# Behind the last FFN tile: 836 further float32r matmuls of four widths, at changing byte offsets between their weights and their moving rows

## The chip, the cores and the metric

The kernel runs on one core of one Trainium2 chip. The metric is the device time of one execution in microseconds. Times of the kernel before: a median of 1186.85 us over 2 runs (1186.52 to 1187.18). One further execution was taken with the hardware profiler; all rows of the profile come from it.

## The reference

The kernel computes one transformer block on 2048 tokens of width 576, with attention and FFN in parallel. Cut to what matters:

```python
x = A_x                                    # (1, 2048, 576) float32
xn = layernorm(x)                          # over the 576 columns, eps 1e-5
qkv = xn @ wqkv                            # 32 heads of 18
o = attention over 8 keys at distances 0, 2, .. 14 behind each token
h = relu(xn @ w1 + b1) ** 2                # 576 -> 4608
out = x + o @ wo + h @ w2 + b2             # 4608 -> 576
```

## The kernel before

**Precision.** A float32 operand is split into a high part in float32r and a float32r rest (`split`, line 96), and a product is made of three matmuls: high by high, high by rest, rest by high. So nearly all work of TensorE is float32r matmuls, each of which appears in the profile as one weight load (engine PEld) and one matmul (engine PE). The first operand of `nc.tensor.matmul` after the destination is the stationary one (128 columns of weights), the second is the moving one, whose number of columns is called the width here.

**Tiling.** The tokens are worked in 4 blocks (`NB`) of 512 (`TB`), and the 4608 hidden columns in 36 tiles of 128 (`NF`). A step n from 0 to 144 (`NT` is 144) does one FFN tile of one block: `step` (line 496) loads the weights of tile n + 2, splits those of n + 1, does `ffn1(n)` and, two steps late (`LAG`), `ffn2(n - 2)`. In steps of its own, listed in `pre` and `mid`, stand the projections to q, k and v (`qkv`, line 243, by `three`, line 235) and the output projection (`o_chunk` and `o_acc`).

**The four widths.** `ffn1` (line 342) has 14 matmuls of width 512 for a tile; `three` (line 241) has 14 of width 432 (`3 * CG`) for 128 tokens; `accumulate` (line 367) has pairs of width 320 (`YA`) and 256 (`YB`), because the 576 output columns are cut into two PSUM segments. In the last step `ffn2_tail` (line 396) does the last two tiles segment by segment, so that there 320 follows 320 and 256 follows 256: for each of six segments it runs all matmuls, then a VectorE addition (`drain`, line 387) and an output DMA.

**Buffers that the change uses.** `raw1` holds the unsplit w1 tile (128 x 640 float32, three buffers, loaded in line 312). `xt` is a single buffer of 10,240 bytes a partition; the normalisation of a block uses it, the last time some steps ahead of the fourth block. `wk` is a pair of PSUM banks, taken in turn by `ffn1`, `three`, and `o_chunk`.

**What sets the order.** A scheduler orders the instructions of each engine from the program's text and its own estimates of time; each engine then runs its list in order, and semaphores hold it where data are missing. Loads and stores are issued by SyncE's queue (SPq in the profile). At the end of the program all engines meet in a barrier, once the last stores have landed.

Of the kernel before, what the change touches and what calls it, by code (L numbers as in the profile page):

```python
# [8 lines left out]
F32 = mybir.dt.float32  # L9
F32R = mybir.dt.float32r  # L10
BF16 = mybir.dt.bfloat16
AF = mybir.ActivationFunctionType
# [4 lines left out]
P = 128  # L17
S, D, F = 2048, 576, 4608
H, DH, W, DIL = 32, 18, 8, 2
TB = 512  # L20
NB = S // TB
NJ = TB // P
NC = 5
# [3 lines left out]
CG = HG * DH  # L27
# [4 lines left out]
YA, YB = 320, 256  # L32
# [8 lines left out]
def block_kernel(ctx: ExitStack, tc: tile.TileContext, x, xt, wqkv, wo, w1, b1, w2, b2, out):  # L41
# [454 lines left out]
    def step(n):  # L496
        if 2 < n + 2 < NT:
            load_w(n + 2)
        if n + 1 < NT:
            split_w1(n + 1)  # L500
        for f, a in pre.get(n, []):
            f(*a)
        if n < NT:
            ffn1(n)
            split_w2(n)
        busy = n >= NF and n % NF in (LAG - 1, LAG - 2)
        for f, a in mid.get(n, []):
            f(*a)
        if not busy:
            piece()  # L510
            piece()
        if n == NT:
            ffn2_tail([NT - 2, NT - 1])
        elif n >= LAG:
            ffn2(n - LAG)
        if not busy:
            piece()

    for n in range(NT + 1):
        with opening() if n < 3 else ExitStack():  # L520
            step(n)


_OUTS = [((1, S, D), 'float32')]

# [33 lines left out]
```

## Time and profile before

| | |
|---|---|
| median of 2 runs | 1186.85 us |
| the profiled execution's own time | 1186.68 us |
| its span, first to last instruction | 1184.6 us |
| PE busy | 1174.9 us, 99% of the span, 6930 matmuls |
| PEld busy | 1080.3 us, 91% |
| VectorE, ScalarE busy | 867.9 us (73%), 596.6 us (50%) |
| mean granted TensorE clock | 0.999 |

A row of the timeline has the start in us, the time it took, engine, line, operation, what is written and read, the shape and how many such instructions were merged into the row. Matmuls are pipelined: the record of one matmul is longer than the distance to the next one's start. What a matmul costs in a stream is therefore read as the distance between starts, or from the chain of waits, where a row gives start, length and number of a piece of work that follows without a gap. The mean ns in the list of groups is the length of the record.

### The profile page before, as it was taken

What the parts mean: (1) busy time and instruction counts of PE and PEld (TensorE: products, weight loads), DVE (VectorE), ACT (ScalarE), POOL (GpSimd) and SP (SyncE); (2) the same over time, 40 slices, a digit from 0 to 9 for tenths busy, and PEclk for the clock granted to TensorE, in tenths of its full rate; (3) what the DMA queues carried; (4) which work ended last, traced back from release to release, by engine and by line L of the source; (5) the groups of instructions that cost most, each with busy time, mean ns of one, the idle gap of its engine ahead of it and who ended that gap; (6) DMA issues with size and microseconds to landing.
All of it is one profiled execution on the core that took longest, in us unless ns stands there. A gap on an engine that the chain in (4) does not pass through costs nothing.

```text
span 1184.6 us, 17735 instructions
## 1 busy us (share of the span) xinstructions
PE 1174.9 (99%) x6930; PEld 1080.3 (91%) x6930; DVE 867.9 (73%) x1051; ACT 596.6 (50%) x1079; POOL 40.3 (3%) x47
## 2 busy tenths in 40 slices
PE   8999999999999999999999999999999999999998
PEld 5999999989999999999989999999999999999998
DVE  7399899882689795994288979598428895958432
ACT  6545445553536454555364545455535454445542
POOL 4003000000000200000000020000000000000000
PEclk9999999999999999999999999999999999999999
DMA  7556345332536554423264654533326434343311
GB/s 239 188 177 220 119 166 201 96 100 78 197 123 212 211 174 144 141 86 116 72 232 133 226 206 125 185 97 106 100 89 227 171 120 172 98 155 96 109 58 50
DMA packets 70164, 172.22 MB, mean 145 GB/s; under 512 B 8384, under 2 KB 20288, under 8 KB 69312
## 3 DMA queue, kind: packets, MB, share of 16 engines
q1 hardware_dynamic: 70080, 171.09, 43.5%
q8 instruction: 54, 0.88, 0.3%
q14 instruction: 30, 0.25, 0.1%
HBM read 156.81 MB, written 14.24 MB: 144 GB/s over the span
## 4 chain that ended last, share of the span: by engine, by line
PE 97%; DVE 2%; issue 0%; ACT 0%; DMA 0%; SPq 0%; POOL 0%; DVEq 0%
PE y L367 43%; PE wk L342 38%; PE wk L241 15%; DVE xt L185 1%; PE wk L202 1%; DVE wql L100 0%; DMA xb<-in_x 0%; SPq L89 0%; PE y L202 0%; DVE w2l L100 0%; DVE hl L349 0%; ACT r L344 0%; ACT hh L347 0%; DVE st L111 0%; DVE w1l L100 0%
## 5 line engine op out<-in xcount | busy, mean ns | idle before, releaser
L367 PE MATMUL y<-w2l,hh 128*128 128x256 f32 (+1 forms) x1152 | 253.1, 296 | 0.0
L367 PE MATMUL y<-w2h,hh 128*128 128x256 f32 (+1 forms) x1152 | 252.8, 297 | 0.0
L367 PE MATMUL y<-w2h,hl 128*128 128x256 f32 (+1 forms) x1152 | 251.8, 296 | 0.0
L342 PE MATMUL wk<-xh,w1h 128*128 128x512 f32 x720 | 213.9, 394 | 0.8 <-DVE kv L207 0.8
L367 PEld LDWEIGHTS y<-w2h,hh 128*128 128x128 f32 x1152 | 186.4, 189 | 7.6
L342 PE MATMUL wk<-xh,w1l 128*128 128x512 f32 x720 | 187.2, 390 | 2.0 <-DVE w1l L100 2.0
L367 PEld LDWEIGHTS y<-w2l,hh 128*128 128x128 f32 x1152 | 180.4, 189 | 1.9
L367 PEld LDWEIGHTS y<-w2h,hl 128*128 128x128 f32 x1152 | 179.8, 190 | 0.5
L98 ACT ACTIVATE w1h<-raw 128x640 fp32r<-128x640 f32 x144 | 106.1, 737 | 120.6 <-PE wk L342 114.6
L98 ACT ACTIVATE w2h<-raw 128x576 fp32r<-128x576 f32 x144 | 98.1, 682 | 134.7 <-PE y L367 134.7
L342 PEld LDWEIGHTS wk<-xh,w1l 128*128 128x128 f32 x720 | 135.1, 188 | 30.3 <-DVE w1l L100 2.3
L342 PE MATMUL wk<-xl,w1h 128*128 128x512 f32 x576 | 155.1, 390 | 0.0
L100 DVE TENSOR_TENSOR w1l<-raw,w1h 128x640 fp32r<-128x640 f32 x143 | 118.9, 832 | 47.7 <-PE wk L342 34.0
L100 DVE TENSOR_TENSOR w2l<-raw,w2h 128x576 fp32r<-128x576 f32 x144 | 110.8, 771 | 55.9 <-ACT w2h L98 55.8
L342 PEld LDWEIGHTS wk<-xh,w1h 128*128 128x128 f32 x720 | 126.2, 189 | 20.5 <-DVE kv L207 1.0
L303 DVE TENSOR_REDUCE qo<-pr 128x144 f32<-128x1152 f32 x64 | 138.8, 2169 | 0.6
L342 PEld LDWEIGHTS wk<-xl,w1h 128*128 128x128 f32 x576 | 108.0, 188 | 23.9
L349 DVE TENSOR_TENSOR hl<-r,hh 128x512 fp32r<-128x512 f32 x144 | 99.5, 691 | 34.1 <-ACT r L348 34.1
L344 ACT ACTIVATE r<-wk,b1t 128x512 f32<-128x512 f32 x144 | 98.5, 684 | 44.5 <-PE wk L342 44.1
L100 DVE TENSOR_TENSOR wql<-wqr,wqh 128x432 fp32r<-128x432 f32 x80 | 50.0, 642 | 95.5 <-ACT wqh L98 95.5
L241 PE MATMUL wk<-wql,xh 128*128 128x432 f32 x320 | 114.8, 359 | 0.0
L241 PE MATMUL wk<-wqh,xh 128*128 128x432 f32 x320 | 114.7, 359 | 0.0
(77 smaller groups left out, 1228.1 us busy)
## 6 DMA issues: line engine op xcount, KB each, us to landing
raw<-in_w SPq DMA_DIRECT2D x144, 320.0 KB, 2.9
raw<-in_w SPq DMA_DIRECT2D x144, 288.0 KB, 2.8
wqr<-in_wqkv SPq DMA_DIRECT2D x80, 216.0 KB, 4.5
kv<-kscr SPq DMA_DIRECT2D x16, 1008.0 KB, 5.3
kv<-vscr SPq DMA_DIRECT2D x16, 1008.0 KB, 7.5
raw<-in_wo SPq DMA_DIRECT2D x20, 288.0 KB, 2.7
kscr<-kv SPq DMA_DIRECT2D x16, 288.0 KB, 3.0
vscr<-kv SPq DMA_DIRECT2D x16, 288.0 KB, 3.4
```

The costliest lines, as they stand in the source:

```text
L98: nc.scalar.activation(hi, raw, AF.Copy)
L100: (only or nc.vector).tensor_tensor(out=lo, in0=raw, in1=hi.bitcast(F32), op=ALU.subtract)
L185: nc.vector.tensor_tensor(out=v, in0=v, in1=mb[b][:, :, k].rearrange("c p j -> c j p"), op=op)
L202: nc.tensor.transpose(p[:, j * P:(j + 1) * P], src[:, j, c * P:(c + 1) * P], ident)
L241: nc.tensor.matmul(ps, l, r, start=i == 0, stop=i == len(mm) - 1)
L303: nc.vector.tensor_reduce(out=q[:, j], in_=pr.rearrange("p w c -> p c w"), axis=AX.X, op=ALU.add)
L342: nc.tensor.matmul(p, l, r, start=i == 0, stop=i == len(mm) - 1)
L344: nc.scalar.activation(r, p, AF.Relu, bias=b1t[:, f:f + 1])
L349: last_hl[0] = nc.vector.tensor_tensor(out=hl, in0=r, in1=hh.bitcast(F32), op=ALU.subtract)
L367: nc.tensor.matmul(y, a[:, t * P:(t + 1) * P], w[:, c0:c1], start=first and i == 0 and opens, stop=last and i == len(pairs) - 1, skip_grou ...
```

## The change

Behind the last step the program gets a new function, called once. It copies the last w1 tile four times into one float32r buffer `t` of 2560 columns, on ScalarE, and then runs matmuls whose weights and moving rows both come from `t`. All write the same PSUM tile `a`, each with start and stop set, and nothing reads `a`. The tokens' output is not touched.

```diff
+    def offset_map():
+        t = sb.tile([P, NC * TB], F32R, name="xt", bufs=1)
+        for i in range(4):
+            nc.scalar.activation(t[:, i * 640:(i + 1) * 640], raw1[NT - 1], AF.Copy)
+        a = pw.tile([P, TB], F32, name="wk")
+
+        def row(w, m, n):
+            nc.tensor.matmul(a[:, :n], t[:, w // 4:w // 4 + P], t[:, m // 4:m // 4 + n],
+                             start=True, stop=True, skip_group_check=True)
+
+        for i in range(4):
+            row(2048, 0, TB)
+        for k in range(32):
+            w = 2048 + 64 * k
+            for n in (TB, 3 * CG, YA, YB):
+                for i in range(4):
+                    row(w, 0, n)
+            for i in range(3):
+                row(w, 0, YA)
+                row(w, 4 * YA, YB)
+        for k in range(8):
+            w = 2560 + 256 * k
+            for n in (TB, 3 * CG, YA, YB):
+                for i in range(4):
+                    row(w, 256, n)
+
+    offset_map()
```

`w` and `m` are byte offsets in a partition's row of `t`. In the first loop `w` takes 32 values, 64 bytes apart, and the moving rows start at 0 (or at 1280, for the second of a pair). In the second loop the moving rows start at 256 and `w` takes 8 values, 256 bytes apart.

In the instruction lists of the changed program, against those of the program before, the 836 matmuls (line 530) stand together at the end of TensorE's list, behind the last matmul of line 367. The four ScalarE copies (line 526) stand earlier: behind the activation of line 348 whose row begins at 1124.60 us in the profile before, ahead of the `w2h` split that begins at 1126.50 us. VectorE, GpSimd and SyncE have the same lists as before.

## The prediction

> **What bounds the kernel now.** First the head of the profile's page, its busy times, the clock, and the shares of the chain of waits; then the chain in order of time, where it shows which rows follow each other without a gap.
>
> ```profile
> span 1184.6 us, 17735 instructions
> PE 1174.9 (99%) x6930; PEld 1080.3 (91%) x6930; DVE 867.9 (73%) x1051; ACT 596.6 (50%) x1079; POOL 40.3 (3%) x47
> PEclk9999999999999999999999999999999999999999
> PE 97%; DVE 2%; issue 0%; ACT 0%; DMA 0%; SPq 0%; POOL 0%; DVEq 0%
> ```
>
> TensorE is busy for 99% of the span and is 97% of the chain, at full granted clock to the end. So a matmul that is put behind the last one isn't absorbed by a gap: it moves the end by its distance to the next start. The chain in order of time, around the steps that matter here and at the end:
>
> ```profile
> 740.46 5.47 PE wk L241 x28
> ```
>
> ```profile
> 1126.47 3.20 PE wk L342 x14
> 1129.67 3.20 PE y L367 x24
> 1132.86 0.44 PE wk L202 x4
> 1133.30 3.20 PE y L367 x24
> 1136.50 3.20 PE wk L342 x14
> 1139.70 3.19 PE y L367 x24
> ...
> 1169.35 11.74 PE y L367 x88
> 1181.10 0.02 issue
> 1181.12 0.49 DVE xb L387
> ```
>
> These rows already price three of the new kinds: width 432 costs 5.47 / 28 = 0.1954 us, width 512 costs 3.20 / 14 = 0.2286 us, and a pair of 320 and 256 costs 3.20 / 12 = 0.2667 us. For 320 behind 320 and 256 behind 256 I read the tail, in the timeline of PE:
>
> ```profile
> 1175.40 0.40 PE L367 MATMUL y<-w2h,hh 128*128 128x256 f32 x2
> ...
> 1176.84 0.31 PE L367 MATMUL y<-w2h,hh 128*128 128x320 f32 x1
> ...
> 1178.60 0.40 PE L367 MATMUL y<-w2h,hh 128*128 128x256 f32 x2
> ...
> 1180.77 0.31 PE L367 MATMUL y<-w2h,hl 128*128 128x320 f32 x1
> ```
>
> By the loops of `ffn2_tail`, 12 matmuls of 256 stand between the first two rows, 12 of 320 between the second and the third: 1.44 / 12 = 0.120 us and 1.76 / 12 = 0.1467 us. The last row is the last matmul of the kernel before; the next could start at 1180.77 + 0.147 = 1180.92.
>
> **A fixed part in every matmul.** From 256 to 320 columns the price grows by 26.7 ns, 0.417 ns a column. With that, 256 columns stream in 106.7 ns and the row of 0.120 us has 13.3 ns over; 320 has 13.3, 512 has 15.3 and 432 has 15.4. Within a group of width 512 it isn't constant:
>
> ```profile
> 1126.30 1.09 PE L342 MATMUL wk<-xh,w1h 128*128 128x512 f32 x4
> 1127.23 1.07 PE L342 MATMUL wk<-xl,w1h 128*128 128x512 f32 x4
> 1128.14 0.39 PE L342 MATMUL wk<-xh,w1h 128*128 128x512 f32 x1
> ```
>
> The first four take 0.93 / 4 = 232.5 ns each (19.2 over), the next four 0.91 / 4 = 227.5 ns (14.2 over). So the part over the stream is 13 to 19 ns and depends on how a load falls against the running matmul. By the built program's addresses the distance from moving rows to weights is a multiple of 256 bytes in all 6816 float32r matmuls of before, and in 308 of the 836 new ones (every fourth k of the first loop, the second loop, the first four). The other 528 (24 x 22) lie at 64, 128 or 192 bytes off that grid, which no row of before shows.
>
> **The 836 matmuls.** 4 + 32 x 22 + 8 x 16. Width 512: 4 + 128 + 32 = 164 x 0.2286 = 37.5 us. Width 432: 160 x 0.1954 = 31.3. Width 320 in fours: 160 x 0.1467 = 23.5. Width 256 in fours: 160 x 0.120 = 19.2. Pairs: 96 x 0.2667 = 25.6. Sum 137.0 us.
>
> For the 528 off the grid the bounds are: below, the whole fixed part of 13.3 ns goes (-7.0 us); above, it is paid twice (+7.0 us), a guess wider than any row. Nearest rows: width 432, whose stream ends off the grid, has 2.1 ns more than 256 and 320; the first four of a 512 group, not yet in step, 5.9 ns more. I take 4 ns, between those two: 528 x 4 = 2.1 us.
>
> **Weights that repeat.** Most new rows have their predecessor's weights. The list of groups shows that this saves no load: in `accumulate` a pair shares its weights, and yet has one load a matmul, 1152 loads for 576 + 576 matmuls.
>
> ```profile
> L367 PEld LDWEIGHTS y<-w2h,hh 128*128 128x128 f32 x1152 | 186.4, 189 | 7.6
> ```
>
> ```profile
> L367 PE MATMUL y<-w2h,hh 128*128 128x320 f32 x576 | 180.3, 313 | 0.0
> ...
> L367 PE MATMUL y<-w2h,hh 128*128 128x256 f32 x576 | 161.0, 281 | 0.0
> ```
>
> **A page on the fixed part.** The Trainium skill, TensorE: Matmul & The Clock Gate, says under "Step-by-step: what each phase is for" that TensorE has two independent SBUF read ports, so that loading the next weights doesn't take read bandwidth from the running matmul, and under "Back-to-back issue gap" gives 2.5 ns over the stream. By it the offset would be nothing, and the sum, an estimate, 125.2 (300,544 columns at 0.417 ns) + 836 x 0.0025 = 127.3 us. The rows above have 13 to 19 ns there, so the trace does not agree on the size; no row of before can show whether the offset is nothing, which is rival A below.
>
> **The four copies on ScalarE.** They wait for the last w1 load, and stand ahead of a `w2h` split:
>
> ```profile
> 1123.78 0.33 SPq L312 DMA_DIRECT2D raw<-in_w  x1
> ```
>
> ```profile
> raw<-in_w SPq DMA_DIRECT2D x144, 320.0 KB, 2.9
> ```
>
> ```profile
> 1124.60 0.63 ACT L348 ACTIVATE r<-r 128x512 f32<-128x512 f32 x1
> 1126.50 0.69 ACT L98 ACTIVATE w2h<-raw 128x576 fp32r<-128x576 f32 x1 [1.28 <-PE y L367]
> 1128.57 0.74 ACT L98 ACTIVATE w1h<-raw 128x640 fp32r<-128x640 f32 x1 [1.38 <-PE wk L342]
> 1129.70 0.69 ACT L344 ACTIVATE r<-wk,b1t 128x512 f32<-128x512 f32 x1 [0.39 <-PE wk L342]
> ```
>
> The load lands at about 1123.78 + 2.9 = 1126.7, the copies run to 1126.7 + 4 x 0.74 = 1129.7. Queued behind them: `w2h` (3.2 us late), `w1h` to 1131.1, r to 1131.8; then VectorE's `w1l`, by about 1132. First to need these is TensorE's next group of line 342 at 1136.50 (row above), for `w1h`, `w1l` and the bank of `wk` that r frees. Cover is 4 us or more, so the copies cost nothing; without it they would cost up to 3.2 us once. SyncE's, GpSimd's and VectorE's lists are not changed, and the new matmuls find `t` ready 50 us ahead.
>
> **The end.** Before, the last store sets it: issued at 1181.64, landing 2.1 us later, 0.9 us ahead of the span's end of 1184.6.
>
> ```profile
> 1181.64 0.34 SPq L410 DMA_DIRECT2D out<-xb  x1
> ```
>
> ```profile
> out<-xb SPq DMA_DIRECT2D x2, 160.0 KB, 2.1
> ```
>
> The last additions and stores now run beside the new matmuls, so 3.7 us behind 1180.92 stop counting. After: 1180.92 + 137.0 + 2.1 (off grid) + 0.16 (the last record is 281 ns long, its distance counted at 120) + 0.9 = 1321.1 us of span. The profiled execution took 1186.68 us, 2.1 more than its span: 1323.2. It stands 0.2 under the median of the runs shown: **1323.4 us**.
>
> **The rivals.**
> - *A, the offset does nothing*: off-grid rows cost what the others do, 1323.4 - 2.1 = 1321.3 us. For it: settled 512 rows have 14 ns wherever on the grid they lie. Against it: no row lies off the grid.
> - *B, off-grid rows are cheaper*: loads and stream stop meeting and up to 13.3 ns fall away in 528 rows, down to 1314.3 us. Against it: in the rows the part over the stream is never under 13.
> - *C, off-grid rows pay the fixed part twice or more*: 1328.3 us and above. For it: the parts of 13 to 19 ns already vary with how a load falls.
> - *D, repeated weights are not loaded again*: the fixed part is gone nearly everywhere, 1321.3 - 836 x 0.0133 = 1310.2 us. The pairs above speak against it.
> - *E, not slower*: `a` is read by nobody; if the matmuls were dropped on the way to the chip, the copies alone would be left and the time stays at 1186.9 us. It decides at the count of PE: 6930 or 7766. The built list has all 836. To hide instead, they would have to fit in the 3.7 us under the last stores, 4.4 ns each, where the cheapest row has 120.
> - *F, the clock halves* in the new stretch: 137 us more, about 1460 us. The clock's row has full speed throughout, and nothing separates the new matmuls from the old.
>
> **How the numbers follow.** Forecast (off-grid rows 2 to 6 ns dearer, 1322.4 to 1324.6): 0.40. A: 0.26. B: 0.14. C: 0.15. D: 0.02. E: 0.01. F: 0.02. The range is 1315 to 1330 us: it takes in the forecast, A, nearly all of B, whose bottom needs every meeting to vanish, and the part of C up to 1.25 times the bound of +7.0 us. Left out are D, E, F, and what of B and C lies beyond: about 0.15. Faster by over 2%: no case, put at 0.00. Within 2% (under 1210.6 us): E, 0.01. Slower by over 2%, which is about what a measurement of this kernel can tell from no change: 0.99.
>
> **What would show it.** Right: PE x7766 and PEld x7766; line 530 in one piece at the end of the chain, starting at about 1180.9, 137 to 141 us long, with as many loads as matmuls; nothing of PE moved around 1126 to 1140, with `w2h` there about 3 us late; the last stores landing near 1183.7 as before; distances of 228, 195, 147 and 120 ns in every fourth k, and a few ns more in the three between. Wrong: distances under 115 ns for 256 columns off the grid (B, or D if on the grid too), over 130 ns (C), a gap of PE ahead of line 530 or near 1136 (a cover that I took for granted), or a clock row under 9 at the end (F).

## The result and the profile after

The changed kernel takes 1320.7 us (median of 2 runs, 1319.95 and 1321.46), against 1186.85 before: a ratio of 1.1128, 95% interval 1.108 to 1.1176. The forecast was 1323.4 us, rival A 1321.3. The profiled execution took 1321.46 us with a span of 1319.4.

The head of the page, the clock, and the shares of the chain by line:

```profile
span 1319.4 us, 19411 instructions
PE 1312.4 (99%) x7766; PEld 1209.4 (92%) x7766; DVE 868.0 (66%) x1051; ACT 598.9 (45%) x1083; POOL 40.1 (3%) x47
PEclk9999999999999999999999999999999999999999
PE y L367 38%; PE wk L342 34%; PE wk L241 13%; PE wk L530 10%; DVE xt L185 1%; PE wk L202 1%; DVE w2l L100 0%; DMA xb<-in_x 0%; SPq L89 0%; DVE wql L100 0%; PE y L202 0%; DVE hl L349 0%; ACT r L344 0%; ACT hh L347 0%; DVE w1l L100 0%
```

TensorE has 836 matmuls and 836 loads more, and the clock stays full. Then the chain in order of time (start, length, what), at the place of the copies and at the end:

```profile
1126.59 3.20 PE wk L342 x14
...
1136.62 3.20 PE wk L342 x14
...
1169.47 11.73 PE y L367 x88
1181.20 137.33 PE wk L530 x836
```

Both groups of line 342 begin 0.12 us later than before (1126.47 and 1136.50), so nothing was lost between them, where the copies stand. The matmuls stand in one piece behind the tail. In the timeline the first of them starts at 1181.04, and the last record ends at 1318.53, 0.9 us ahead of the span's end as summed. That is 137.5 us, where the forecast had 137.0 + 2.1 + 0.16 = 139.3 and rival A 137.2. (The chain counts the piece from the end of the last record before it, so its 137.33 is nearly the sum of the distances, to be held against 137.0.)

The copies, in the timeline of ScalarE:

```profile
1126.63 2.62 ACT L526 ACTIVATE xt<-raw 128x640 fp32r<-128x640 f32 x4 [1.28 <-DMA raw<-in_w]
1129.15 0.67 ACT L98 ACTIVATE w2h<-raw 128x576 fp32r<-128x576 f32 x1
```

They wait for the load as predicted; `w2h` begins 2.65 us later than before (1126.50), not 3.2, because four copies back to back take 2.6 us.

### The profile page after: what moved, and what is told of

Same layout as the page of the kernel before. It is cut to its first block, busy times and chain, and to the rows that moved or that the text cites. A ratio compares the mean times of both kernels' runs of the same rounds, so it can differ in the third digit from the quotient of the medians.

```text
span 1319.4 us, 19411 instructions
## 1 busy us (share of the span) xinstructions
PE 1312.4 (99%) x7766; PEld 1209.4 (92%) x7766; DVE 868.0 (66%) x1051; ACT 598.9 (45%) x1083; POOL 40.1 (3%) x47
## 4 chain that ended last, share of the span: by engine, by line
PE 97%; DVE 2%; ACT 0%; DMA 0%; issue 0%; SPq 0%; POOL 0%; DVEq 0%
PE y L367 38%; PE wk L342 34%; PE wk L241 13%; PE wk L530 10%; DVE xt L185 1%; PE wk L202 1%; DVE w2l L100 0%; DMA xb<-in_x 0%; SPq L89 0%; DVE wql L100 0%; PE y L202 0%; DVE hl L349 0%; ACT r L344 0%; ACT hh L347 0%; DVE w1l L100 0%
## 5 line engine op out<-in xcount | busy, mean ns | idle before, releaser
L530 PE MATMUL wk<-xt 128*128 128x320 f32 (+3 forms) x836 | 137.5, 327 | 0.0
L530 PEld LDWEIGHTS wk<-xt 128*128 128x128 f32 x836 | 129.0, 188 | 8.4
```

The lines of the kernel that those rows point to most:

```text
L530: nc.tensor.matmul(a[:, :n], t[:, w // 4:w // 4 + P], t[:, m // 4:m // 4 + n], start=True, stop=True, skip_group_check=True)
```

## The experiments

Theories. *Forecast*: a row off the grid of 256 bytes costs 4 ns more. *A*: the offset does nothing; it moves time between neighbours, the sum stays. *Settled price*: each width has a price of its own at each offset, which a long stretch of that width shows, and the mix of the change hides it.

**The copies alone** (e1_copies). The matmuls are left out.

```diff
-        a = pw.tile([P, TB], F32, name="wk")
...
```

> The four ScalarE copies alone, none of the 836 matmuls. If the copies are covered, as predicted: 1186.9 us, within 0.5 of the kernel before, w2h about 2.6 us later there and the line 342 group after it in its place. If the cover is gone in part: up to 3.2 us more, 1190.1, with a gap of PE near 1136 us.

Measured: 1185.96 us (11 runs) beside 1186.75 of the kernel before; ratio 0.9998, interval 0.9989 to 1.0007. The copies cost nothing, to within the 1 us of that interval; all of the change's time is that of the matmuls.

**All rows on the grid, all rows off it** (e2_on_grid, e3_off_grid). Only `w` is changed; the second diff is shown for the loops, its first four rows have 2112 in place of 2048.

```diff
-            w = 2048 + 64 * k
+            w = 2048 + 256 * (k % 8)
```

```diff
-            w = 2048 + 64 * k
+            w = 2048 + 256 * (k % 8) + 64 * (1 + k % 3)
...
-            w = 2560 + 256 * k
+            w = 2560 + 256 * k + 64 * (1 + k % 3)
```

> The same 836 matmuls, but every w lies a multiple of 256 bytes from the moving rows. The changed kernel took 1320.7 us. By the forecast (off-grid rows 4 ns dearer, 528 of them gone): 1318.6 us. By rival A (the offset shifts time only between the rows of a group, the sum stays): 1320.7, within 0.8. If each offset has a settled price of its own that groups of four hide: no sum is given by it, but a difference to the off-grid kernel of over 2 us would speak for it.

> The same 836 matmuls, but every w lies 64, 128 or 192 bytes off the grid. By the forecast: 308 more rows 4 ns dearer, 1321.9 us, 3.3 more than the kernel with all rows on the grid. By rival A: 1320.7, within 0.8, and the two kernels equal within 0.5.

Measured: 1321.3 us on the grid (ratio to before 1.1133, interval 1.1118 to 1.1148) and 1321.68 off it (1.1135, 1.112 to 1.115). The chain has the piece alone, first on the grid, then off it:

```profile
1181.74 137.97 PE wk L530 x836
```

```profile
1181.79 137.13 PE wk L530 x836
```

The forecast wanted 3.3 us more off the grid; the piece is 0.84 us shorter there. The medians of the whole can't decide so little, since the five runs on the grid alone spread over 2 us; the starts in the two traces can. One k of the first loop, 22 matmuls, takes 3.585 to 3.588 us on the grid from the second k on, and 3.559 to 3.571 off it. The forecast's term falls, with the wrong sign.

The same starts show why all rows on the grid cost more than the sum's 137.0: a four of 512 behind the pairs takes 0.930 us there, 232 ns a row, as the first four of a 512 group did before, and not 228.6. And in the changed kernel a k on the grid takes only 3.568 us from k = 4 on, with 0.916 or 0.917 for its four of 512. At `w` = 2304 these are the same matmuls on the same columns of `t` in both kernels; only the rows ahead differ, on the grid in one and 192 bytes off it in the other. So the price of a group of four still depends on what stands ahead of it. A and the settled price stay open.

**Long stretches of one width at one offset** (e4_long). In place of the loops stand 18 stretches of 48 matmuls, each with a line of its own; two of them:

```diff
+        for i in range(48):  # 512 at 0
+            nc.tensor.matmul(a[:128, :512], t[:, 512:512 + 128], t[:, 0:0 + 512], start=True, stop=True, skip_group_check=True)
+        for i in range(48):  # 512 at 64
+            nc.tensor.matmul(a[:128, :512], t[:, 528:528 + 128], t[:, 0:0 + 512], start=True, stop=True, skip_group_check=True)
...
```

> Stretches of 48 matmuls of one width at one offset: widths 512, 432, 320, 256, each at 0, 64, 128 and 192 bytes off the grid, and then 512 and 256 with weights that alternate between two places. By rival A each stretch costs 48 x (width x 0.4167 + 13.3 ns), 432 some 2 ns a row more, whatever the offset: 10.9, 9.4, 7.0, 5.8 us, and alternating weights the same. If each offset has a settled price of its own that groups of four hid, stretches of one width differ by 2 to 9 ns a row, 0.1 to 0.45 us a stretch. If repeated weights are cheaper than new ones, the alternating stretches are longer.

Measured: 1333.19 us. The chain in order of time; lines 530 to 536 are width 512 at 0, 64, 128 and 192 bytes, 538 to 544 width 432, 546 to 552 width 320, 554 to 560 width 256, and 562 and 564 alternate their weights at 512 and 256:

```profile
1181.12 10.90 PE wk L530 x48
1192.02 11.20 PE wk L532 x48
1203.22 11.16 PE wk L534 x48
1214.38 10.99 PE wk L536 x48
1225.38 9.40 PE wk L538 x48
1234.78 9.30 PE wk L540 x48
1244.08 9.39 PE wk L542 x48
1253.46 9.40 PE wk L544 x48
1262.86 7.04 PE wk L546 x48
1269.91 7.04 PE wk L548 x48
...
1291.02 5.75 PE wk L554 x48
1296.77 5.46 PE wk L556 x48
1302.23 5.69 PE wk L558 x48
1307.92 5.65 PE wk L560 x48
1313.58 10.93 PE wk L562 x48
1324.50 5.75 PE wk L564 x48
```

Divide by 48 and take off the stream (0.4167 ns a column): width 512 has 13.8 ns over at 0 and 20.0, 19.2 and 15.6 off the grid; width 256 has 13.1 at 0 and 7.1, 11.9 and 11.0 off it; 432 gains 2 ns at 64 alone; 320 has 13.3 wherever it lies. So the offset does have a price, of opposite sign for 512 and for 256: A in its plain form falls as well. Over the four widths at equal number, 192 matmuls take 33.09 us at 0 and 33.00, 33.28 and 33.08 at the others: at most 0.19 us, 1 ns a matmul, is left in the sum. Alternating weights cost what repeated ones cost.

**The same rows, a line for each width** (e11_lines). Order and addresses are those of the change, and only the source lines differ:

```diff
+            for i in range(4):
+                nc.tensor.matmul(*at(w, m, TB), **f)
+            for i in range(4):
+                nc.tensor.matmul(*at(w, m, 3 * CG), **f)
...
```

> The 836 matmuls of the changed kernel in the same order at the same addresses, only written out so that each width has a source line of its own. 1320.7 us, within 1. By rival A in its plain form (a row costs the same at any offset): every four of 512 takes the same time at each k, and so with the other widths. By what the long stretches settled at: the four of 512 is 15 to 20 ns longer at 64, 128 and 192 bytes than at 0, 256 and the pairs are shorter there by about as much, and only their sum is the same, 3.56 to 3.57 us for each k.

Measured: 1321.56 us. The chain from k = 0 (at 0 bytes), then of k = 1 (64 bytes) the first and last piece, and the first of k = 2 and of k = 3; line 536 is width 512, 542 is 256, 551 the pairs:

```profile
1182.22 0.91 PE wk L536 x4
...
1184.51 0.48 PE wk L542 x4
1184.99 0.80 PE wk L551 x6
1185.79 0.93 PE wk L536 x4
...
1188.56 0.79 PE wk L551 x6
1189.35 0.93 PE wk L536 x4
...
1192.91 0.94 PE wk L536 x4
```

The chain rounds to 10 ns; the starts in the trace are finer, and every fourth k, 256 bytes on, repeats them to within 2 ns from k = 4 on. The four of 512 takes 0.917 us on the grid and 0.927, 0.932 and 0.932 at 64, 128 and 192 bytes, 2.5 to 4 ns a row more. The four of 256 takes 0.477, and 5 to 6 ns less off the grid; the pairs take 0.800, and 7 to 12 ns less (0.792 at 128). A whole k takes 3.568, 3.569, 3.560 and 3.568 us. So inside the change, too, gains and losses nearly cancel. But the 0.917 is not the price of the grid alone: with all rows on the grid the same four takes 0.930, as much as off it.

**Finer offsets, fewer columns, bfloat16.** Three more kernels of long stretches. e5_fine has 512 and 256 at 0, 4, 8, 16, 32 and 36 bytes (`t[:, 513:...]` is 4 bytes). e6_columns loads 128, 96, 64 and 32 columns of weights. e7_bf16 makes `t` bfloat16, with twice as many columns and eight copies:

```diff
-        t = sb.tile([P, NC * TB], F32R, name="xt", bufs=1)
+        t = sb.tile([P, 2 * NC * TB], BF16, name="xt", bufs=1)
...
```

> Stretches of 48 matmuls, width 512 and then 256, at 0, 4, 8, 16, 32 and 36 bytes off the grid of 256. Settled prices so far: 512 takes 13.3 ns over its stream at 0 and 20.0 at 64; 256 takes 13.2 at 0 and 6.8 at 64. If the weights and the moving rows meet by lines of 16 bytes: 4 and 8 bytes as at 0 (10.9 and 5.75 us a stretch), 16 and 32 off by some ns a row. If by blocks of 64 bytes: all six as at 0. If the price follows the byte distance smoothly: each one between those at 0 and 64.

> Stretches of 48 matmuls at offset 0, width 512 and then 256, with 128, 96, 64 and 32 columns of weights; the result then has as many partitions. If the part over the stream is the price of reading the weights beside the moving rows, it falls with the columns: 13.3, 10, 6.7, 3.3 ns a row, stretches of 10.9, 10.7, 10.6, 10.4 us and 5.75, 5.6, 5.4, 5.3 us. If it is a switch of weights that has one price, all stretches of a width are alike.

> The buffer in bfloat16, 128 columns of weights, stretches of 48 of widths 512, 432, 320, 256, each at 0 and 64 bytes. If the part over the stream comes from reading float32 weights beside float32 moving rows, it shrinks with half the bytes or goes: 2 to 7 ns, stretches of 10.3 to 10.6 us at width 512 and 5.2 to 5.5 at 256, and the offset does little. If it is a switch with one price: 13 ns, 10.9 and 5.75 us.

Measured: 1285.34, 1250.42 and 1245.96 us. First e5_fine, width 512 at 0, 4 and 8 bytes (lines 530 to 534) and 256 at 0, 4 and 8 (542 to 546); the fence behind it is e6_columns, 512 and 256 with 128 and 32 columns; the last e7_bf16, 432 at 0 and 64, 256 at 0 and 64:

```profile
1181.49 10.91 PE wk L530 x48
1192.40 11.16 PE wk L532 x48
1203.56 11.07 PE wk L534 x48
...
1248.23 5.74 PE wk L542 x48
1253.97 5.68 PE wk L544 x48
1259.65 5.56 PE wk L546 x48
```

```profile
1181.16 10.91 PE wk L530 x48
...
1214.15 11.12 PE wk L536 x48
1225.27 5.76 PE wk L538 x48
...
1242.05 5.44 PE wk L544 x48
```

```profile
1201.99 8.76 PE wk L534 x48
1210.75 8.76 PE wk L536 x48
...
1232.55 5.24 PE wk L542 x48
1237.79 5.24 PE wk L544 x48
```

Four bytes already change the price: 5.2 ns a row more at 512. So neither lines of 16 bytes nor blocks of 64 are the unit, and the price isn't smooth either. With a quarter of the columns 256 gets cheaper by 6.7 ns, but 512 dearer by 4.4: the part over the stream is not in proportion to the weights read, and it is not one fixed price. In bfloat16 it is 2.5 ns (8.76 / 48 - 0.180, 5.24 / 48 - 0.1067) and does not move with the offset. But a bfloat16 load is also shorter (a record of 98 ns against 188), so this run doesn't part the bytes from the length of the load. What holds a float32r matmul up is not settled: the offset alone moves it, but no run shows what meets what.

**Pairs as the FFN has them** (e8_pairs), 24 pairs at each of 16 offsets.

```diff
+        for i in range(24):  # pairs at 128
+            for m, n in ((0, YA), (4 * YA, YB)):
+                nc.tensor.matmul(a[:, :n], t[:, 544:544 + P], t[:, m // 4:m // 4 + n], start=True, stop=True, skip_group_check=True)
...
```

> 24 pairs of width 320 and 256 on the same weights, as the FFN's second matmul has them, at 16 offsets, 16 bytes apart. At 0: 24 x 0.2667 = 6.40 us. In the changed kernel three pairs at 128 took some 15 ns less than at 0, 5 ns a pair: 6.28 us there, if groups of three show the settled price; all 16 between 6.1 and 6.5. If pairs settle at one price whatever the offset, 6.40 in all 16.

Measured: 1286.13 us. Line 531 is 0 bytes, 534 is 16, 555 is 128, 558 is 144:

```profile
1181.46 6.40 PE wk L531 x48
1187.86 6.37 PE wk L534 x48
...
1232.40 6.24 PE wk L555 x48
1238.64 6.40 PE wk L558 x48
```

All 16 lie between 6.24 and 6.41 us, the least at 128: 6.7 ns a pair under the grid's price, and 16 bytes further on nothing of it is left.

**The offset in the kernel itself** (e9_shift, e10_w1_off). Nothing is added to the kernel before; operands are moved in wider buffers, and the lists of all engines stay the same. In e9_shift `w2h`, `w2l`, and likewise `woh` and `wol`, begin at 128 bytes; in line 367 they are the moving rows (the expectation calls them weights), and `hh`, `hl` and `kv` are the weights. In e10_w1_off `w1h` and `w1l` begin at 64; they are the weights of line 342.

```diff
-        hi = mt.tile([P, D], F32R, name="w2h", bufs=3)
-        lo = mt.tile([P, D], F32R, name="w2l", bufs=3)
+        hi = mt.tile([P, D + 64], F32R, name="w2h", bufs=3)[:, 32:32 + D]
+        lo = mt.tile([P, D + 64], F32R, name="w2l", bufs=3)[:, 32:32 + D]
...
```

```diff
-            w1s[n] = (mt.tile([P, NC * P], F32R, name="w1h", bufs=2),
-                      mt.tile([P, NC * P], F32R, name="w1l", bufs=2))
+            w1s[n] = (mt.tile([P, NC * P + 64], F32R, name="w1h", bufs=2)[:, 16:16 + NC * P],
+                      mt.tile([P, NC * P + 64], F32R, name="w1l", bufs=2)[:, 16:16 + NC * P])
```

> The kernel before, without the added matmuls, but w2h, w2l, woh and wol begin 128 bytes into their buffers, so that all 3904 matmuls of 320 and 256 columns have their weights 128 bytes off the grid. If the price that long stretches of pairs settle at (6.24 us for 24 pairs at 128 bytes, 6.40 at 0) holds in the kernel: 3904 x 3.3 ns = 13 us less, about 1174 us. If only what groups of three pairs showed in the changed kernel holds, 2.5 ns a matmul: about 1177. If the price in the kernel's own order, with new weights at each pair, doesn't depend on the offset: 1186.7, within 0.6.

> The kernel before, without the added matmuls, but w1h and w1l begin 64 bytes into their buffers: the 2016 matmuls of width 512 have their weights 64 bytes off the grid. By the settled price of that offset (20.0 ns over the stream against 15.3 in the kernel's groups of 14): 2016 x 4.7 ns = 9.5 us more, about 1196 us, groups of line 342 of 3.27 us instead of 3.20. If the offset does nothing over a mixed sequence, as rival A has it: 1186.7, within 0.6.

Measured: 1177.65 us with the pairs at 128 bytes (ratio to before 0.992, interval 0.9907 to 0.9932) and 1195.46 us with width 512 at 64 (1.0072, 1.0058 to 1.0086); the kernel before took 1187.11 beside them. The chain, of e9_shift a plain step and one with transposes in it, of e10_w1_off one group:

```profile
1005.49 3.17 PE wk L342 x14
1008.66 3.14 PE y L367 x24
...
1111.72 3.20 PE wk L342 x14
1114.92 0.44 PE wk L202 x4
1115.36 3.20 PE y L367 x24
```

```profile
1126.54 3.27 PE wk L342 x14
```

In e9_shift the 24 matmuls of a tile take 3.14 us where they took 3.20 (3.19 in most steps), and the group of 512, whose own offset is unchanged, 3.17 where it took 3.20. In most steps behind transposes (line 202) the 24 keep their 3.20. Added up from the starts in the two profiled executions, 8.4 us apart, the 3904 moved matmuls give 6.2 us, 1.6 ns each, and the 2016 of line 342 give 3.0 us. The change's own pairs at 128 bytes show 1.4 ns a matmul (0.800 and 0.792 us for six), not the 2.5 of the expectation. So the 9.5 us between the medians met the expected 1177 by luck: the pairs bring less, and the 512 groups behind them bring the rest, which no expectation had. Why they do is open. The 13 us of the long stretches, where the weights stay, are not reached. In e10_w1_off the group takes 3.27 us as expected, and the whole 8.4 us more where 9.5 were expected. So in the kernel's own order the offset does move the time, and e9_shift takes 0.8% less than the kernel before.

## Why the prediction was right, and which step of it failed

- *TensorE sets the end, and what is put behind it counts in full*: right. 836 matmuls, one piece, full clock.
- *Prices by width from the rows of before, 137.0 us*: right within 1%, and 1.0 us too low for rows that all lie on the grid (137.97). The largest part, 0.6 us, is width 512: it was priced at the mean of a group of 14, 228.6 ns, but the new rows come in fours, and a row of the prediction itself had 232.5 ns for the first four. That the change's own piece is 137.33 us, so near to 137.0, is partly luck, because the rows off the grid took 0.64 us off again.
- *Repeated weights are loaded again, at the same price* (against D): right; 836 loads, and alternating weights cost 10.93 us a stretch where repeated ones cost 10.90.
- *The copies cost nothing*: right, by the kernel that has them alone. The lateness was 2.65 us, not 3.2, since the sum took 0.74 us for each copy and four in a row overlap.
- *The end*: right. 0.9 us behind the last matmul, 2.1 us around the span.
- *The step that failed: "I take 4 ns, between those two: 528 x 4 = 2.1 us."* The two rows that it stands between, 432 and the first four of a 512 group, both have their weights on the grid, so neither showed what the offset does. With all rows on the grid the piece takes 137.97 us, in the change 137.33, with all rows off it 137.13: the offset takes about 1 ns a row off instead of adding 4. By width, in fours, off against on the grid: 256 and the pairs get cheaper, 320 and 432 stay within 0.5 ns a row or get up to 2 ns cheaper, and 512 takes 0.924 to 0.932 us where it has 0.930 in the kernel that is all on the grid. So this term was 2.7 us too high and the sum of prices 1.0 too low, which leaves 1.8 in the piece. The rest of the forecast's 2.7 us is within the 1.5 us between the two runs.
- *"Depends on how a load falls against the running matmul"*: not shown. The runs show that the price moves with the offset and with the rows ahead; none shows the load as the cause.
- *Against B: "the part over the stream is never under 13"*: wrong as a general statement. It held for the rows of before, which lie on the grid; 256 at 64 bytes has 7.1 ns.
- *A* gave the right time, 1321.3 us, but its reason, that the offset does nothing, is refuted by the long stretches and by the two kernels with moved operands. It was right by a balance of the mix and by a sum of prices that was too low by about as much as the offset gave back.

The page of the Trainium skill that the prediction weighed, TensorE: Matmul & The Clock Gate, section "Back-to-back issue gap", gives 2.5 ns over the stream at the full clock, for what it calls the isolated gap. For bfloat16 the runs agree to the tenth, in a stream with a load for each matmul (182.5 ns for 432 columns, 109.2 for 256); for float32r the long stretches have 7 to 20 ns, and the measurement decides.

## What to carry to other kernels

Where TensorE is the bound, price a new matmul by the distance of starts of its own width in its own kind of sequence: fours of 512 behind pairs cost 232 ns where groups of 14 had 228.6, and the sum here came out 1.0 us under the 138.0 of the rows on the grid. An unknown that can have either sign for different shapes must not get one size for all of them; take it by shape, or leave it at nothing with a range. And a flat sum over a mixed probe does not show that a parameter is without effect: here long stretches found up to 6 ns a row under it, and moving `w2h`, `w2l`, `woh` and `wol` by 128 bytes brought 9.5 us of 1187.

## What the runs showed of the hardware that was not expected

- The price of a float32r matmul depends on the byte distance between its moving rows and its weights: in long stretches at 64 bytes 512 columns cost 6.2 ns more and 256 columns 6.0 ns less than at 0. Four bytes are enough for 5.2 ns at 512. In the change the prices repeat every 256 bytes, eight times over. Pairs gain at 128 bytes when the weights are moved (e8_pairs) and when the moving rows are (e9_shift), which speaks for the distance and against either address alone.
- Fewer columns of weights can make a matmul slower: 512 columns of moving rows take 227.3 ns with 128 columns of weights and 231.7 with 32.
- In bfloat16 no such dependence appears: 2.5 ns over the stream at both offsets tried (0 and 64 bytes, widths 432 and 256).
- The sequence ahead counts: 14 matmuls of 512 at an unchanged offset took 3.17 us behind moved pairs and 3.20 behind the old ones, and a four of 512 on the same columns of `t` 0.930 us behind pairs on the grid and 0.916 behind pairs 192 bytes off it.
